# Dividing one late weight transfer into 100 and 28 rows, and moving a one-number load to GpSimd's queue

## The chip, the cores and the metric

The kernel runs on one core of a Trainium2 chip. The metric is device time in microseconds, the median of several executions. A profile of one more execution comes with it; it names the engines PE (TensorE, with PEld for its weight loads), DVE (VectorE), ACT (ScalarE), POOL (GpSimd) and SP (SyncE), and the sixteen DMA engines that move data between main memory and the core's on-chip memory.

## The reference

The computation is one decoding step for two sequences (batch 2, one token each, width 512): a normalised input goes through attention over a window of a cached key and value store, and the result is multiplied by a gate from a small gated network.

```python
xn = layernorm(x)                                     # x: (2, 1, 512)
# attention: 32 query heads, 8 key/value heads, head size 128, the last 4096 of 32768 cached rows
q = (xn @ wq)                                         # wq: (512, 4096)
p = softmax(q k^T * 128 ** -0.5);  o = p v            # k, v: (2, 8, 4096, 128) of the caches
s = o.reshape(2, 1, 4096) @ wo                        # wo: (4096, 512)
# gate
z = gelu(xn @ w_in)                                   # w_in: (512, 1792); z1, z2: halves of 896
g = silu((z1 * (w_sp * layernorm(z2) + b_sp)) @ w_out)  # w_sp, b_sp: one number each; w_out: (896, 512)
out = x + s * g
```

All numbers are 32-bit floats. The windows of k and v are 64 MB together, wq and wo 8 MB each, w_in 3.5 MB and w_out 1.75 MB (MB of 2^20 bytes here).

## The kernel before

Almost all loads are issued by SyncE, in the order of the code: `win`, `wout`, two halves of `wq`, then the eight units (one key/value head each, both sequences) of 4 MB of k and 4 MB of v, interleaved, and at the end eight pieces of `wo`. The large tiles share a ring of four slots of 4 MB; a load into a slot waits until the engine that read the slot's former tile is done. ScalarE issues three small loads at the start (`xs`, the two rows of x, and the two numbers w_sp and b_sp into the tile `wb1`) and the store of the result at the end. GpSimd issues one load, x in another layout (`x4`), after it has cleared that tile, and then prepares constants (`ident`, `selw`, `xnT` and others). The order on TensorE, VectorE, ScalarE and SyncE is that of the code (`InOrder`).

For each unit VectorE transposes the keys in four chunks (`turn`, tiles `kt`), TensorE makes the scores (`scores`), a few short steps on VectorE, TensorE and ScalarE turn them into probabilities (`probabilities`), and TensorE multiplies them with the values (`values`, tile `acc`). The heads' outputs are collected in three sets, of units 0 to 3, 4 and 5, and 6 and 7 (`SETS`), each spread into a tile `oT`.

Each set has its part of `wo`, viewed as 128 rows of 16, 8 and 8 blocks of 512 numbers. It is loaded in pieces: set 0 in two pieces of 8 blocks (2 MB each), set 1 in two of 4 blocks (1 MB each), and set 2 in pieces of 4, 2, 1 and 1 blocks (1 MB, 512 KB, 256 KB, 256 KB). In the code a piece is named by its set `i` and first block `j`; the last but one piece is (2, 6), the last (2, 7). In each piece of one block a row is 2 KB. The products of the first four pieces go to `part`, which is summed into `so`; the products of set 2 are added to `so` directly, piece by piece as they land (the loop over `blocks` from 4 on). Two VectorE instructions then make the result `res`, and ScalarE stores it.

The framework gives each transfer of SyncE and ScalarE one of eight completion counters, in rotation, and a transfer waits until the one before it on its counter has landed.

Of the kernel before, what the change touches and what calls it, by code (L numbers as in the profile page):

```python
# [14 lines left out]
P = 128  # L15
# [27 lines left out]
def kernel(  # L43
# [13 lines left out]
    nc = tc.nc  # L57
    pe, dve, act, sp = (InOrder(tc, e) for e in (nc.tensor, nc.vector, nc.scalar, nc.sync))
# [24 lines left out]
    def slot(name, *shape):  # L83
        return ring.tile([P, *shape], F32, tag="slot", name=name)
# [14 lines left out]
    for a in range(0, KT, 2):  # L99
        t = slot(f"wq{a}", 2, HQ * DH)  # L100
# [1 line left out]
        wqt += [t[:, 0], t[:, 1]]  # L102

    wb1 = cst.tile([1, 2], F32, tag="wb1", name="wb1")
    act.dma_start(wb1[:, 0:1], bass.AP(tensor=w_sp.tensor, offset=w_sp.offset, ap=[[1, 1], [1, 1]]))
    act.dma_start(wb1[:, 1:2], bass.AP(tensor=b_sp.tensor, offset=b_sp.offset, ap=[[1, 1], [1, 1]]))
    x4 = cst.tile([P, DC], F32, tag="x4", name="x4")
    nc.gpsimd.memset(x4, 0.0)
# [381 lines left out]
        scores(cur, 0, 1, 2, 3)  # L490


    wo_s = []
    for kv, n, nj in SETS:
        r0, r1 = kv * REP * DH, (kv + n) * REP * DH
# [2 lines left out]
    for first, of in ((0, (0,)), (1, (1, 2))):  # L498
        t = slot(f"wo{first}", 16, D)
        a = 0  # L500
        for i in of:
            nj = SETS[i][2]
            for j, n in (((0, 8), (8, 8)), ((0, 4), (4, 4)), ((0, 4), (4, 2), (6, 1), (7, 1)))[i]:
                sp.dma_start(t[:, a : a + n, :], wo_s[i][:, j : j + n, :])
                blocks.append((t[:, a : a + n, :], sets[f"oT{i}"][1], j))
                a += n
    EARLY = 24
# [30 lines left out]
    for n in range(4, len(blocks)):  # L538
        t, oT, j = blocks[n]
# [38 lines left out]
```

## Time and profile before

| | |
|---|---|
| median of 3 runs | 218.35 us (218.16 to 218.53) |
| profiled execution | 218.31 us |
| its span, first to last instruction | 216.1 us |
| granted TensorE clock, mean | 0.832 |
| PE / DVE / ACT / POOL busy | 135.0 / 104.9 / 24.0 / 4.0 us |
| read from main memory | 89.40 MB, 414 GB/s over the span |

The profile's times are of one execution and count from its first instruction. A row of an instruction group names its engine, its operation, what it writes and reads (out<-in, buffer numbers left out) and its shape; "idle before" or a bracket is the time in which the engine stood idle just before, and what ended it. Rows of instructions that go through `InOrder` all carry its line, L37. An engine's name with a q means its instruction queue: "SPq DMA_DIRECT2D" is the issue of a transfer, not the transfer. DMA queues are numbered: q1 is SyncE's, q10 ScalarE's, q0 GpSimd's, q8 and q14 carry instructions. In a table of windows each row has the stretch, its length, for each engine the busy time and number of instructions, the granted TensorE clock, the busy share of the sixteen DMA engines and GB/s.

### The profile page before, as it was taken

To read this page: it belongs to the slowest core of one execution; us is meant where nothing else is said; L and a number is where in the kernel's file an instruction comes from. 1 tells how busy PE (TensorE), PEld (TensorE's weight loads), DVE (VectorE), ACT (ScalarE), POOL (GpSimd) and SP (SyncE) were. 2 spreads that over 40 slices of the span, in tenths; PEclk is the share of its full clock that TensorE was granted. 3 is DMA by queue.
4 is the path that set the end of the run, shared out by engine and by line. 5 is a ranking of instruction groups with operands and counts; after the bars stand their busy time and mean duration, and the time that the engine had idled before them with its cause. 6 is when DMAs were issued, how large, how long until landed. Compare 5 with 4: busy or idle time off the path is not lost.

```text
span 216.1 us, 2106 instructions
## 1 busy us (share of the span) xinstructions
PE 135.0 (62%) x862; PEld 42.8 (20%) x862; DVE 104.9 (49%) x161; ACT 24.0 (11%) x60; POOL 4.0 (2%) x20
## 2 busy tenths in 40 slices
PE   0173294627774993973594199179567489968653
PEld 0120021113111221320131023033111122342221
DVE  2604014439539539658508910885784684511201
ACT  4103003200001021101021002012000012031010
POOL 7000000000000000000000000000000000000000
PEclk9998569995588598796589559959966969999998
DMA  7999999999999999999999999999999999999990
GB/s 255 425 437 455 418 455 418 429 431 418 455 400 461 403 455 418 443 425 425 443 421 443 406 449 425 449 425 428 437 418 449 400 456 409 443 409 417 417 373 25
DMA packets 4092, 89.52 MB, mean 414 GB/s; under 512 B 486, under 2 KB 498, under 8 KB 884
## 3 DMA queue, kind: packets, MB, share of 16 engines
q1 hardware_dynamic: 4032, 89.39, 96.7%
q8 instruction: 6, 0.10, 0.2%
q14 instruction: 2, 0.02, 0.0%
q10 hardware_dynamic: 20, 0.01, 0.0%
q0 software_dynamic: 32, 0.00, 0.0%
HBM read 89.40 MB, written 0.00 MB: 414 GB/s over the span
## 4 chain that ended last, share of the span: by engine, by line
DMA 71%; PE 13%; DVE 12%; SPq 1%; ACT 1%; issue 1%; ACTq 0%; DVEq 0%
DMA v<-in_A_v_cache_dram 42%; DMA k<-in_A_k_cache_dram 20%; DMA wo<-in_A_wo_dram 9%; DVE kt L37 8%; PE acc L37 7%; PE s L37 3%; PE pp L37 2%; SPq L37 1%; ACT p L37 1%; DVE pT L37 1%; DVE sm L37 1%; DVE qw L37 1%; DVE both L37 0%; PE col L37 0%; DVE res L37 0%
## 5 line engine op out<-in xcount | busy, mean ns | idle before, releaser
L37 DVE STREAM_TRANSPOSE kt<-k 128x2048 f32<-128x2048 f32 x32 | 72.5, 2286 | 3.5 <-DMA k<-in_A_k_cache_dram 3.5
L37 PE MATMUL acc<-v,pT 128*32 128x512 f32 x256 | 40.1, 781 | 11.4 <-DMA v<-in_A_v_cache_dram 10.5
L37 PE MATMUL s<-kt,qw 128*32 128x512 f32 x256 | 39.8, 669 | 4.6 <-DVE kt L37 4.1
L37 PE MATMUL pp<-p,swap 128*128 128x512 f32 x16 | 12.4, 871 | 21.3 <-ACT p L37 21.3
L37 DVE CUSTOM_DVE_ANT_1 sm<-s,own 128x512 f32<-128x512 f32 x8 | 5.5, 692 | 34.2 <-PE s L37 34.2
L37 PEld LDWEIGHTS acc<-v,pT 128*32 128x32 f32 x256 | 10.5, 152 | 39.4 <-issue 35.6
L37 PE MATMUL q_ps<-wq,xnT 128*32 128x512 f32 x64 | 9.7, 732 | 11.0 <-DMA wq<-in_A_wq_dram 11.0
L37 ACT ACTIVATE o<-acc,diag 128x128 f32<-128x128 f32 x30 | 8.7, 369 | 69.3 <-PE acc L37 68.9
L37 PEld LDWEIGHTS s<-kt,qw 128*32 128x32 f32 x256 | 9.5, 120 | 34.0 <-issue 20.8
L37 ACT ACTIVATE p<-sm,nb 128x512 f32<-128x512 f32 x8 | 5.8, 725 | 70.8 <-DVE nb L37 70.8
L37 DVE TENSOR_TENSOR lsum<-pl,diag 128x4 f32<-128x4 f32 x3 | 0.5, 162 | 16.7 <-PE pl L37 16.7
L37 DVE STREAM_TRANSPOSE pT<-pp 128x512 f32<-128x512 f32 x8 | 5.7, 714 | 5.7 <-PE pp L37 5.6
L37 PE MATMUL z<-win,xnT 128*32 128x448 f32 x32 | 5.7, 887 | 3.9 <-DMA win<-in_B_w_in_dram 3.9
L37 PE MATMUL part<-wo,oT 128*32 128x512 f32 x48 | 6.0, 600 | 2.8 <-DMA wo<-in_A_wo_dram 2.8
L37 PE MATMUL col<-o,selw 128*32 128x128 f32 (+1 forms) x28 | 7.6, 436 | 0.0
L37 PEld LDWEIGHTS pp<-p,swap 128*128 128x128 f32 x16 | 2.8, 218 | 22.0 <-ACT p L37 22.0
L37 PE MATMUL mo<-mg,same 128*128 128x16 f32 x16 | 3.2, 273 | 5.8 <-DVE mg L37 5.3
L37 DVE TENSOR_TENSOR res<-so,gate 128x128 f32<-128x128 f32 x1 | 0.3, 292 | 10.4 <-PE so L37 10.4
L37 ACT ACT_TABLE_LOAD x4 | 5.1, 1283 | 2.0 <-issue 1.9
L37 PE MATMUL xnT_ps<-ident,xn 2*128 2x2 f32 x4 | 0.6, 252 | 7.5 <-DVE xn L37 7.5
L37 PE MATMUL qj_ps<-qT,selj 128*128 128x64 f32 x8 | 2.0, 428 | 4.9 <-DVE qT L37 4.9
L37 PEld LDWEIGHTS q_ps<-wq,xnT 128*32 128x32 f32 x64 | 2.0, 126 | 14.6 <-DMA wq<-in_A_wq_dram 11.1
(110 smaller groups left out, 65.0 us busy)
## 6 DMA issues: line engine op xcount, KB each, us to landing
k<-in_A_k_cache_dram SPq DMA_DIRECT2D x8, 4096.0 KB, 23.4
v<-in_A_v_cache_dram SPq DMA_DIRECT2D x8, 4096.0 KB, 31.2
wq<-in_A_wq_dram SPq DMA_DIRECT2D x2, 4096.0 KB, 28.9
wo<-in_A_wo_dram SPq DMA_DIRECT2D x2, 2048.0 KB
win<-in_B_w_in_dram SPq DMA_DIRECT2D x1, 3584.0 KB, 11.1
wo<-in_A_wo_dram SPq DMA_DIRECT2D x3, 1024.0 KB, 23.2
wout<-in_B_w_out_dram SPq DMA_DIRECT2D x1, 1792.0 KB, 15.0
wo<-in_A_wo_dram SPq DMA_DIRECT2D x1, 512.0 KB, 26.9
```

Source lines behind the costliest of these rows:

```text
L37: return self.tc.keep_in_program_order(call(*args, **kwargs))
```

## The change

The piece (2, 6) of wo is loaded by two transfers, one of its rows 0 to 99 and one of rows 100 to 127, in place of one transfer of 128 rows. The load of w_sp, a single number, is issued by GpSimd instead of ScalarE; in GpSimd's order it stands first, ahead of the clearing of x4. The destinations are the same. The matmuls of the piece now wait for both transfers.

```diff
     wb1 = cst.tile([1, 2], F32, tag="wb1", name="wb1")
-    act.dma_start(wb1[:, 0:1], bass.AP(tensor=w_sp.tensor, offset=w_sp.offset, ap=[[1, 1], [1, 1]]))
+    nc.gpsimd.dma_start(wb1[:, 0:1], bass.AP(tensor=w_sp.tensor, offset=w_sp.offset, ap=[[1, 1], [1, 1]]))
     act.dma_start(wb1[:, 1:2], bass.AP(tensor=b_sp.tensor, offset=b_sp.offset, ap=[[1, 1], [1, 1]]))
...
+    LATE = ((2, 6),)
     wo_s = []
...
             for j, n in (((0, 8), (8, 8)), ((0, 4), (4, 4)), ((0, 4), (4, 2), (6, 1), (7, 1)))[i]:
-                sp.dma_start(t[:, a : a + n, :], wo_s[i][:, j : j + n, :])
+                deal = ((0, 100), (100, P)) if (i, j) in LATE else ((0, P),)
+                for p0, p1 in deal:
+                    sp.dma_start(t[p0:p1, a : a + n, :], wo_s[i][p0:p1, j : j + n, :])
                 blocks.append((t[:, a : a + n, :], sets[f"oT{i}"][1], j))
```

## The prediction

> **What bounds the kernel now.** I read the page first, for the engines, the DMA share and the queues.
>
> ```profile
> span 216.1 us, 2106 instructions
> ...
> DMA  7999999999999999999999999999999999999990
> ...
> ## 3 DMA queue, kind: packets, MB, share of 16 engines
> q1 hardware_dynamic: 4032, 89.39, 96.7%
> q8 instruction: 6, 0.10, 0.2%
> q14 instruction: 2, 0.02, 0.0%
> q10 hardware_dynamic: 20, 0.01, 0.0%
> ...
> DMA 71%; PE 13%; DVE 12%; SPq 1%; ACT 1%; issue 1%; ACTq 0%; DVEq 0%
> ```
>
> The sixteen DMA engines are busy in every slice but the first and the last, and 96.7% of their time goes to one queue, SyncE's. The kernel is bound by the loading of its 89 MB. What ends it is the chain's last part:
>
> ```profile
> 192.53 19.79 DMA wo<-in_A_wo_dram
> ...
> 212.37 0.47 PE so L37 x8
> ...
> 212.87 0.30 DVE res L37
> ...
> 213.19 0.29 DVE res L37
> ```
>
> The last piece of wo lands at 192.53 + 19.79 = 212.32 us. Behind it stand eight matmuls and two VectorE instructions, which the change leaves alone, and then the store and the closing barriers to 216.1. So the time moves with the landing of the last piece, us for us, as long as nothing else becomes late. The profiled execution took 218.31 us, 2.2 us more than its span; I keep these 2.2 us, and the median of the runs, 218.35, is only 0.04 above it.
>
> A transfer has landed when the slowest of its engines has finished. The third view is a table of short windows over the last microseconds, whose last two columns are the busy share of the sixteen engines and GB/s:
>
> ```profile
> 209.60:209.90 0.30, 0.00 (x0) 0.02 (x1) 0.00 (x0) 0.00 (x0) 0.00 (x0) 1.00 0.97 369
> 209.90:210.20 0.30, 0.28 (x12) 0.30 (x16) 0.00 (x0) 0.00 (x0) 0.00 (x0) 1.00 0.60 232
> 210.20:210.50 0.30, 0.30 (x22) 0.30 (x14) 0.00 (x0) 0.00 (x0) 0.00 (x0) 1.00 0.59 225
> 210.50:210.80 0.30, 0.30 (x20) 0.23 (x10) 0.00 (x0) 0.00 (x0) 0.00 (x0) 1.00 0.54 205
> 210.80:211.10 0.30, 0.22 (x12) 0.03 (x4) 0.00 (x0) 0.00 (x0) 0.00 (x0) 1.00 0.46 171
> 211.10:211.40 0.30, 0.30 (x12) 0.30 (x16) 0.00 (x0) 0.00 (x0) 0.00 (x0) 1.00 0.39 150
> 211.40:211.70 0.30, 0.30 (x12) 0.05 (x4) 0.00 (x0) 0.00 (x0) 0.00 (x0) 1.00 0.19 68
> 211.70:212.00 0.30, 0.28 (x11) 0.16 (x8) 0.00 (x0) 0.00 (x0) 0.00 (x0) 1.00 0.02 7
> ```
>
> The engines do not finish together. Some six to eight are done by 210.2 (share 0.6 and then 0.54), the others run on alone, and the last stops after 211.7. Nor does an engine speed up when others stop: 205 GB/s on 0.54 x 16 = 8.6 engines is 23.7 GB/s each, 150 on 0.39 x 16 = 6.2 is 24.0. The area under the shares from 209.9 on is 0.30 x (0.60+0.59+0.54+0.46+0.39+0.19+0.02) = 0.84 us, so sixteen equally loaded engines would all stop at about 210.75 instead of 211.8. About 1.1 us is what any new dealing of the last pieces could gain at most. The queue table names a cause for half of the engines being late: six packets of instructions on queue 8 (0.10 MB, some 16 KB each) and two on queue 14, eight in all, push themselves between the data. If each fell on another engine, eight engines are behind, as the share of 0.54 says, six of them by more.
>
> **The change part by part: the split piece.** How a transfer is dealt out can be counted.
>
> ```profile
> L37 SPq DMA_DIRECT2D k<-in_A_k_cache_dram x8: 534/535/610, 3.0 to 130.8; - x8
> L37 SPq DMA_DIRECT2D v<-in_A_v_cache_dram x8: 534/535/557, 32.3 to 164.3; - x8
> L37 SPq DMA_DIRECT2D wo<-in_A_wo_dram x8: 328/427/1549, 180.7 to 192.5; - x8
> L37 SPq DMA_DIRECT2D wq<-in_A_wq_dram x2: 430/654/877, 1.6 to 2.1; - x2
> L37 SPq DMA_DIRECT2D win<-in_B_w_in_dram x1: 363/363/363, 0.7 to 0.7; - x1
> L37 SPq DMA_DIRECT2D wout<-in_B_w_out_dram x1: 420/420/420, 1.2 to 1.2; - x1
> ```
>
> These are 28 transfers of 128 rows, and 4032 packets are 28 x 16 x 9: each of sixteen engines gets eight rows and one packet more, which must be its completion. The ACT queue's 20 packets fit the same: two rows on two engines (2 + 2), two single numbers (2 x 2), and the output's eight rows on four engines (8 + 4). So rows go evenly to as many engines as divide them. 128 = 16 x 8; 100 has no divisor between 10 and 16, so 10 x 10; 28 = 14 x 2. If both begin at the first engine, engines 1 to 10 get 12 rows of the piece where they had 8, engines 11 to 14 get 2, engines 15 and 16 none. No trace here shows a transfer of 100 rows, so this is an estimate from those counts.
>
> [...]
>
> One row of this piece is 2 KB. Its price comes from the two last pieces, of eight rows an engine each:
>
> ```profile
> 211.07 0.38 PEld L37 LDWEIGHTS so<-wo,oT 128*32 128x32 f32 x16 [0.35 <-DMA wo<-in_A_wo_dram]
> 211.73 0.16 PEld L37 LDWEIGHTS so<-wo,oT 128*32 128x32 f32 x8 [0.28 <-DMA wo<-in_A_wo_dram]
> 212.37 0.16 PEld L37 LDWEIGHTS so<-wo,oT 128*32 128x32 f32 x8 [0.48 <-DMA wo<-in_A_wo_dram]
> ```
>
> The waits for them end at 211.73 and 212.37, 0.64 us apart: 0.08 us a row. (23.7 GB/s an engine would make it 0.086; I take 0.08, the direct reading.) Engines 1 to 10 thus become 4 x 0.08 = 0.32 us later, 11 to 14 become 6 x 0.08 = 0.48 us earlier, 15 and 16 become 0.64 us earlier.
>
> What this does to the end depends on which engines are late, and no view numbers them. If the six hit by queue 8 are the six that are relieved, the last packet moves from 211.8 to about 211.35; the two hit by queue 14, which I put at 211.0 where the share falls from 0.46 to 0.39, move to 211.35 too, and the punctual ones from at most 210.5 to 210.8. The end comes 0.45 us earlier. If the very last engine is one of the first ten, it comes 0.32 us later. Those are the two ends for the split: -0.64 (the last two engines alone being late) to +0.32. I take -0.45: eight packets and eight late engines mean that instruction packets go round the engines instead of returning to one, so a round of six may well fall on six neighbours; and if every queue with little to carry begins at the first engine, as I assumed for these transfers, the low places are less likely to be the late ones. That is a judgement which no row settles, and it gets little more than half of the chances.
>
> TensorE can follow: before 211.73 its weight loads sat idle for 0.28 us and before 212.37 for 0.48 us, both on DMA, so the last eight matmuls could begin up to about 0.7 us earlier. Both halves of the split piece must land before its matmuls. On every engine its share of both halves still comes before its share of the last piece, so the last piece remains the one that ends.
>
> **SyncE's queue.** One more issue costs 0.43 us (median of the wo row) on an engine that only waits. By the order of the built program the completion counters are used in rotation, eight of them; with one more transfer on SyncE the second half waits for the last v, and the last piece waits for the first wo, where before it waited for the last v and went out at 192.5.
>
> ```profile
> 197.45 1.92 PE L37 MATMUL part<-wo,oT 128*32 128x512 f32 x16 [0.63 <-DMA wo<-in_A_wo_dram]
> ```
>
> The first wo ends a wait at 197.45, so the last piece is issued some 5 us later than now and 12 us before the engines begin to run out of work at 209.6. The 6 MB ahead of it cover this: it costs nothing unless that wait lasted to about 208.
>
> **The moved load.** GpSimd issues it ahead of everything else it does; ScalarE has one issue fewer at its start.
>
> ```profile
> 0.74 0.20 POOL L108 MEMSET x<- 128x128 f32 x1 [0.29 <-POOLq L564]
> ...
> 1.30 0.68 POOL L110 DMA_DIRECT2D x<-in_A_x_dram  x1 [0.21 <-POOL ident masks.py:197]
> ...
> 2.41 0.37 DVE L37 TENSOR_REDUCE rowm<-ident 128x32 f32<-128x128 f32 x1 [2.41 <-POOL ident masks.py:199]
> ...
> 11.96 0.23 PEld L37 LDWEIGHTS z<-win,xnT 128*32 128x32 f32 x8 [3.92 <-issue]
> 17.62 0.38 PE L37 MATMUL wb_ps<-wb,ones 1*128 1x2 f32 x2
> ...
> DMA to landing us min/median/max: 6.5/6.5/6.5
> ```
>
> By GpSimd's one issue, 0.68 us, all its memsets, the identity and the load of x4 slip by 0.7 us; behind them waits VectorE's first reduction (2.41) and then the normalised x. TensorE idles 3.92 us before its first use of win, which covers 0.7 us. The number itself lands about 0.74 + 6.5 = 7.2 us (6.5 is what GpSimd's present load of x takes), ten before the matmul at 17.62 that reads it. On the DMA engines a few bytes move from one queue to another; I book 0, within 0.02 us either way. If the cover in front of win were gone, it would cost 0.7 us in the head, still behind a queue with the next loads already in it.
>
> **The sum.** -0.45 (split) + 0 (issues) + 0 (moved load): 218.31 - 0.45 = 217.86 for an execution like the profiled one, 217.9 beside the median of 218.35. About 0.2%, 0.44 us, is what a measurement of this kernel can tell from no change, so even the likeliest case lies on that line.
>
> **The rivals.**
> First, slower: the slowest engine is one of the first ten. Then its 12 rows end 0.32 us later: 218.35 + 0.32 = 218.67. It decides as soon as a single engine among the ten ends within 0.45 us of the last. For it speaks that only six places in sixteen are relieved, so a round of six that starts one engine earlier puts the first-hit engine among the ten; against it that the shares after 211.1 (0.39) show just six engines left, as many as are relieved. [...]
> Second, the split does nothing: the rows are dealt to all engines after all (7 at most and 2, one row more on some: +0.08), or the late engines change from execution to execution and the two signs cancel: 218.35 to 218.45. The three times, 218.16 to 218.53, lie close, which says little either way.
> Third, a confined transfer is worse than counted: as the output's eight rows took four engines, 100 rows could go to four, 25 rows each: 17 more than now, 17 x 0.08 = 1.4 us, so 219.7. Against it stands that the output's other side has only four leading rows.
>
> **How the numbers follow.** Forecast 0.55, slowest among the ten 0.28, nothing 0.09, narrower dealing 0.05, 0.03 for a loss elsewhere. Within the forecast the gain runs from 0.3 to 0.64, and I put 0.38 beyond the line of 0.44 and 0.17 inside. Of the first rival 0.21 stays inside, 0.07 goes beyond. Faster 0.38; same 0.17 + 0.21 + 0.09 = 0.47; slower 0.07 + 0.05 + 0.03 = 0.15. The forecast alone reaches from 217.7 to 218.1; the range of eight in ten goes on to 218.8, over the first rival with its spread, and leaves out the narrower dealing.
>
> **What would show it.** In the changed kernel's windows the share should stay above 0.6 to about 210.6 and then fall within 0.8 us, instead of a tail of 1.9 us; the last two waits on DMA for wo should end about 211.3 and 211.9. Packets of SyncE's queue should be 4032 - 144 + 128 + 10 + 14 = 4040 (two transfers in place of one, 128 rows and 10 + 14 completions), and fewer if fewer engines take part. The forecast is wrong if the last wait ends after 212.37, or if the tail is as long as before.

## The result and the profile after

The changed kernel takes 219.41 us (median; 218.83 to 219.62). The kernel before, run beside it on the same chip, takes 218.53 us (217.71 to 219.09). The ratio is 1.0037, with a 95% interval of 1.0020 to 1.0055: slower by 0.4 to 1.2 us, 0.8 in the middle (the two medians differ by 0.88). The prediction was 217.9 us with a range to 218.8, so it was wrong, on the other side of no change and past the end of the range.

The page of the changed kernel, in the parts that were shown of before:

```profile
span 217.0 us, 2109 instructions
...
DMA  7999999999999999999999999999999999999990
...
## 3 DMA queue, kind: packets, MB, share of 16 engines
q1 hardware_dynamic: 4040, 89.39, 96.8%
q8 instruction: 6, 0.10, 0.2%
q0 software_dynamic: 64, 0.00, 0.0%
q14 instruction: 2, 0.02, 0.0%
q10 hardware_dynamic: 18, 0.01, 0.0%
```

The page hardly differs. SyncE's queue has 4040 packets, the number that was worked out from 10 and 14 engines, and the slices of the DMA engines look as they did. The span is 0.9 us longer. The end of its chain of work shows where (start, duration, what):

```profile
192.40 20.27 DMA wo<-in_A_wo_dram
...
212.80 0.86 PE so L37 x16
...
213.68 0.30 DVE res L37
```

The chain still ends with wo, the matmuls and the result. The transfer that it names, however, is not the last piece. By the order of the code it is the second part of the split piece, rows 100 to 127, which goes out at 192.40 and lands at 212.67. Behind it SyncE has to wait, in a wait that its list of waits before does not have (engine and line, what it waited for, us in total, times, longest):

```profile
SPq L37 <- DMA wo<-in_A_wo_dram: 4.6, 1, 4.6
```

So the last piece goes out at 197.31, where it went out at 192.53 before, and lands 15.8 us later, at 213.1. That is the later issue that the prediction had worked out for it. The chain joins the last sixteen matmuls; the waits in the timeline separate the pieces of wo (start, busy, tile, and in brackets the idle time before and its releaser):

```profile
211.78 0.38 PEld L37 LDWEIGHTS so<-wo,oT 128*32 128x32 f32 x16 [1.02 <-DMA wo<-in_A_wo_dram]
...
212.77 0.19 PEld L37 LDWEIGHTS so<-wo,oT 128*32 128x32 f32 x8 [0.61 <-DMA wo<-in_A_wo_dram]
...
213.19 0.16 PEld L37 LDWEIGHTS so<-wo,oT 128*32 128x32 f32 x8 [0.23 <-DMA wo<-in_A_wo_dram]
```

Before, these three waits ended at 211.07, 211.73 and 212.37. They are now later by 0.71, 1.04 and 0.82 us. The first of them is for the piece of 512 KB that stands ahead of the split piece in the queue, and the change does not touch it. So most of the loss is there before the split piece is needed at all. A dealing of rows that is merely uneven does not do that: in the run with 40 added rows, below, rows queued behind a piece left the waits for the pieces ahead of them where they were (211.02 and 211.66 against 211.07 and 211.73). That engines which had already reached the rows of the split piece slowed down the others is an inference; the windows fit it, though no view shows one engine apart from the others (last two columns: busy share of the sixteen engines, GB/s):

```profile
209.30:209.60 0.30, 0.10 (x4) 0.00 (x0) 0.00 (x0) 0.00 (x0) 0.00 (x0) 1.00 1.06 253
...
209.60:209.90 0.30, 0.00 (x0) 0.00 (x0) 0.00 (x0) 0.00 (x0) 0.00 (x0) 1.00 1.05 239
209.90:210.20 0.30, 0.25 (x9) 0.28 (x13) 0.00 (x0) 0.00 (x0) 0.00 (x0) 1.00 0.93 259
210.20:210.50 0.30, 0.30 (x21) 0.30 (x16) 0.00 (x0) 0.00 (x0) 0.00 (x0) 1.00 0.90 205
210.50:210.80 0.30, 0.30 (x20) 0.26 (x11) 0.00 (x0) 0.00 (x0) 0.00 (x0) 1.00 0.98 253
210.80:211.10 0.30, 0.23 (x11) 0.00 (x0) 0.00 (x0) 0.00 (x0) 0.00 (x0) 1.00 0.84 212
211.10:211.40 0.30, 0.00 (x0) 0.00 (x0) 0.00 (x0) 0.00 (x0) 0.00 (x0) 1.00 0.77 225
211.40:211.70 0.30, 0.00 (x0) 0.00 (x0) 0.00 (x0) 0.00 (x0) 0.00 (x0) 1.00 0.53 191
211.70:212.00 0.30, 0.22 (x8) 0.22 (x12) 0.00 (x0) 0.00 (x0) 0.00 (x0) 1.00 0.35 130
212.00:212.30 0.30, 0.30 (x16) 0.16 (x8) 0.00 (x0) 0.00 (x0) 0.00 (x0) 1.00 0.14 48
```

Read the two last columns together. The share stays near 1 to 210.8, which looks like the even finish that was hoped for. But the bytes do not go with it. Divided by 16 times the share, the rate of a busy engine is 14.2 GB/s at 209.6 (239 / 16.8), 17.4, 14.2, 16.1, 15.8, 18.3, and only from 211.4 on 22.5 and 23.2. Before, it was 23.2 to 24.2 up to 211.4. From 209.3 to 210.8, for 1.5 us, nearly every engine was busy (share 0.90 to 1.06) and moved 14.2 to 17.4 GB/s, some 60 to 75% of its rate before.

### The profile page after: what moved, and what is told of

Its sections match the earlier page's. It is cut to its first block, busy times and chain, and to the rows that moved or that the text cites. A ratio compares the mean times of both kernels' runs of the same rounds, so it can differ in the third digit from the quotient of the medians.

```text
span 217.0 us, 2109 instructions
## 1 busy us (share of the span) xinstructions
PE 136.5 (63%) x862; PEld 42.4 (20%) x862; DVE 104.8 (48%) x161; ACT 24.0 (11%) x60; POOL 4.7 (2%) x21
## 3 DMA queue, kind: packets, MB, share of 16 engines
q1 hardware_dynamic: 4040, 89.39, 96.8%
## 4 chain that ended last, share of the span: by engine, by line
DMA 72%; PE 13%; DVE 11%; issue 1%; SPq 1%; ACT 0%; ACTq 0%; DVEq 0%
DMA v<-in_A_v_cache_dram 42%; DMA k<-in_A_k_cache_dram 20%; DMA wo<-in_A_wo_dram 9%; DVE kt L37 9%; PE acc L37 8%; PE s L37 4%; SPq L37 1%; PE pp L37 1%; DVE sm L37 1%; DVE qw L37 1%; DVE pT L37 1%; PE so L37 0%; ACT p L37 0%; DVE res L37 0%; DVE mg L37 0%
## 5 line engine op out<-in xcount | busy, mean ns | idle before, releaser
L37 PE MATMUL s<-kt,qw 128*32 128x512 f32 x256 | 40.3, 655 | 4.2 <-DVE kt L37 2.9
L37 PE MATMUL q_ps<-wq,xnT 128*32 128x512 f32 x64 | 10.7, 801 | 12.4 <-DMA wq<-in_A_wq_dram 12.4
L37 PE MATMUL part<-wo,oT 128*32 128x512 f32 x48 | 7.4, 725 | 1.8 <-DMA wo<-in_A_wo_dram 1.7
L37 PE MATMUL z<-win,xnT 128*32 128x448 f32 x32 | 4.9, 776 | 3.6 <-DMA win<-in_B_w_in_dram 3.6
L37 PEld LDWEIGHTS mo<-mg,same 128*128 128x128 f32 x16 | 2.4, 188 | 11.9 <-DVE mg L37 11.9
```

The source lines that it names most:

```text
L37: return self.tc.keep_in_program_order(call(*args, **kwargs))
```

## The experiments

Two theories stood at the start. **Crowding** (theory A in the expectations): while the rows of the split piece are written, engines get in each other's way, and lose part of their rate. **Uneven rows** (theory B): by the prediction's count ten engines have 12 rows where they had 8, and one of them is last; that can cost at most the 0.32 us of the prediction's first rival. Beside them stood the moved load (theory C) and the second transfer as such (theory D). In the diffs below, lines with a minus are those of the changed kernel, `P` is 128 and `D` is 512. Every kernel but the first keeps the moved load.

**The two halves of the change, each alone.** The split without the moved load:

```diff
-    nc.gpsimd.dma_start(wb1[:, 0:1], bass.AP(tensor=w_sp.tensor, offset=w_sp.offset, ap=[[1, 1], [1, 1]]))
+    act.dma_start(wb1[:, 0:1], bass.AP(tensor=w_sp.tensor, offset=w_sp.offset, ap=[[1, 1], [1, 1]]))
```

> The split alone, the number's load stays on ScalarE. Theory A (crowding: while the 100 and 28 rows are written, the engines get in each other's way and every packet takes longer): all of the loss is the split's, so about 0.8 us slower than before, the last wait for wo ends near 213.2 us, and between 209.6 and 211.1 us a busy engine moves 14 to 17 GB/s where it moved 24. Theory B (uneven rows alone: ten engines have four rows more): also the split's, but at most 4 x 0.08 = 0.32 us, and a busy engine keeps 24 GB/s. Theory C (the moved load costs it): no loss, within 0.2 us of before.

Measured: 219.37 us (219.06 to 220.74) against 218.16, ratio 1.0061 (1.0036 to 1.0086). The moved load without the split:

```diff
-    LATE = ((2, 6),)
+    LATE = ()
```

> The moved load alone, the piece whole. Theories A and B: within 0.2 us of before, the last wait for wo ends near 212.4 us, first use of win at 12.0 to 12.3 us. Theory C: about 0.8 us slower, as the changed kernel.

Measured: 218.08 us (217.95 to 218.78) against 218.16, ratio 1.0001 (0.9988 to 1.0014). The windows of the split alone, and then the last waits of the moved load alone:

```profile
209.10:209.40 0.30, 0.00 (x0) 0.00 (x0) 0.00 (x0) 0.30 (x1) 0.00 (x0) 0.50 1.05 253
...
209.60:209.90 0.30, 0.15 (x4) 0.15 (x8) 0.00 (x0) 0.10 (x1) 0.00 (x0) 0.50 1.04 239
```

```profile
211.11 0.38 PEld L37 LDWEIGHTS so<-wo,oT 128*32 128x32 f32 x16 [0.36 <-DMA wo<-in_A_wo_dram]
211.76 0.16 PEld L37 LDWEIGHTS so<-wo,oT 128*32 128x32 f32 x8 [0.27 <-DMA wo<-in_A_wo_dram]
212.41 0.16 PEld L37 LDWEIGHTS so<-wo,oT 128*32 128x32 f32 x8 [0.49 <-DMA wo<-in_A_wo_dram]
```

With the split alone the engines are full (1.05) at 15.1 GB/s each; with the moved load alone the waits end within 0.04 us of before. The whole loss is the split's. (In the profile of the split alone the granted TensorE clock was 0.50 at the end, so its last waits are not compared.)

**Even shares, two contiguous halves.** If uneven rows were the cause, 64 + 64 rows would cost nothing, since 64 divides into sixteen fours and by the same count every engine has eight rows again.

```diff
-                deal = ((0, 100), (100, P)) if (i, j) in LATE else ((0, P),)
+                deal = ((0, 64), (64, P)) if (i, j) in LATE else ((0, P),)
```

> The piece in rows 0 to 63 and 64 to 127: every engine gets 4 + 4 rows, as many as in one transfer, so the rows are even. Theory A, in the form that an engine gets consecutive rows and that rows near each other share a way into the memory: each half crowds into half of the ways, 8 rows take up to 16 x 0.08 us, so 0.4 to 0.7 us slower than before, and GB/s per busy engine falls to 12 to 16 while it lasts. [...] Theory B: rows are even, so within 0.1 us of before, 24 GB/s per busy engine. Theory D (a second transfer as such costs it, by its issue, its counter or its completion): as the changed kernel, 0.8 us slower, with 24 GB/s.

Measured: 219.06 us (218.52 to 220.49) against 218.16, ratio 1.0043 (1.0023 to 1.0063). Windows and two waits of it:

```profile
209.10:209.40 0.30, 0.30 (x8) 0.12 (x8) 0.00 (x0) 0.00 (x0) 0.00 (x0) 1.00 0.88 225
209.40:209.70 0.30, 0.10 (x4) 0.00 (x0) 0.00 (x0) 0.00 (x0) 0.00 (x0) 1.00 1.05 225
```

```profile
212.00 0.38 PEld L37 LDWEIGHTS so<-wo,oT 128*32 128x32 f32 x16 [0.88 <-DMA wo<-in_A_wo_dram]
...
212.87 0.46 PEld L37 LDWEIGHTS so<-wo,oT 128*32 128x32 f32 x16 [0.49 <-DMA wo<-in_A_wo_dram]
```

SyncE's queue has 4048 packets, which has room for the 128 rows of the piece and 32 completions: sixteen engines for each half, so eight rows of the piece for each. A busy engine moves 16.0 and 13.4 GB/s. The untouched piece ahead is 0.93 us late (212.00 against 211.07). Uneven rows alone are out as the main cause. The loss, 0.5 to 1.4 us by the interval, is if anything larger than the 0.4 to 0.7 us that crowding was given.

**Uneven shares without the split.** The piece stays whole, and a transfer of 40 rows into a tile that nobody reads follows it: by the prediction's count, 40 = 10 x 4, ten engines get 12 rows in all and the other six keep 8.

```diff
-                for p0, p1 in deal:
-                    sp.dma_start(t[p0:p1, a : a + n, :], wo_s[i][p0:p1, j : j + n, :])
+                sp.dma_start(t[:, a : a + n, :], wo_s[i][:, j : j + n, :])
+                if (i, j) in LATE:
+                    extra = cst.tile([P, 1, D], F32, tag="extra", name="extra")
+                    sp.dma_start(extra[32:72], wo_s[i][32:72, j : j + n, :])
```

> [...] Theory A: no crowding, 24 GB/s per busy engine; the end moves by 0.32 us if the slowest engine is one of the ten, and by 0 to 0.1 us if the slowest are the other six. Theory B (uneven rows cost it all): as the changed kernel, 0.8 us. Theory D: 0.8 us as well.

Measured: 218.38 us (217.97 to 219.48) against 218.16, ratio 1.0013 (0.9998 to 1.0028). Its last waits and a window:

```profile
211.02 0.38 PEld L37 LDWEIGHTS so<-wo,oT 128*32 128x32 f32 x16 [0.38 <-DMA wo<-in_A_wo_dram]
211.66 0.16 PEld L37 LDWEIGHTS so<-wo,oT 128*32 128x32 f32 x8 [0.26 <-DMA wo<-in_A_wo_dram]
212.63 0.16 PEld L37 LDWEIGHTS so<-wo,oT 128*32 128x32 f32 x8 [0.82 <-DMA wo<-in_A_wo_dram]
```

```profile
210.50:210.80 0.30, 0.30 (x16) 0.15 (x7) 0.00 (x0) 0.00 (x0) 0.00 (x0) 1.00 0.60 225
...
212.00:212.30 0.30, 0.08 (x4) 0.00 (x0) 0.00 (x0) 0.00 (x0) 0.00 (x0) 1.00 0.02 7
```

The rate is the old one (225 / 9.6 = 23.4), and the two waits ahead of the last end where they did before (211.07 and 211.73): rows queued behind a piece do not delay it by themselves. The gap between the last two waits is 0.97 us instead of 0.64. That is 0.33 us more, the size that the first rival gave four rows, so in this execution the last engine seems to be among the ten. A share of 0.02 over 0.3 us is 0.1 us of one engine's time, so hardly more than one is left there. That is the size of the uneven rows: 0.3 us, not 0.8.

**Which of the ten.** The piece stays whole, and 8, 9 or 10 rows of 8 KB (four blocks each, to places of `wout` that have been used) follow it, one on each of as many engines if they are dealt as counted: four prices of a 2 KB row on each of 8, 9 or 10 engines. That these are always the first ones is an assumption; no view numbers the engines. The lines stand behind the transfer of the whole piece; with nine and ten rows the slice ends at 68 and 72.

```diff
...
+                if (i, j) in LATE:
+                    some = slice(32, 64, 4)
+                    sp.dma_start(wout[some, 0:4, :], wo_s[i][some, 0:4, :])
```

> [...] It asks where the slowest engine sits: 8 KB take about 0.31 us. The time between the ends of the last two waits for wo is 0.64 us without it. If the slowest engine is one of the first eight it becomes 0.95 us; if all the late ones stand behind the eighth, it stays 0.64 to 0.7 us.

> The same with 9 rows (32, 36 to 64), one for each of the first nine engines. If the gap between the last two waits is 0.95 us here and 0.64 us with eight rows, the slowest engine is the ninth.

> The same with 10 rows (32, 36 to 68), one for each of the first ten engines. The 40 extra rows gave a gap of 0.97 us, so 0.95 us is expected here; 0.64 us would mean that the slowest engine changes from execution to execution. If eight and nine rows leave the gap at 0.64 us and this one makes it 0.95 us, the slowest is the tenth, just inside the ten that the change loads more.

Measured, one time each beside 218.58 of before: 218.23, 218.43 and 218.23. The last waits with eight rows:

```profile
211.40 0.16 PEld L37 LDWEIGHTS so<-wo,oT 128*32 128x32 f32 x8 [0.27 <-DMA wo<-in_A_wo_dram]
212.31 0.16 PEld L37 LDWEIGHTS so<-wo,oT 128*32 128x32 f32 x8 [0.76 <-DMA wo<-in_A_wo_dram]
```

The gap is 0.91 instead of 0.64, so in this execution the last engine seems to be among the eight that got a row more. With nine and ten rows it could not be read, since TensorE came to these pieces later than they landed and waited for none of them. These two are inconclusive.

**A second transfer without other rows.** Two transfers of all 128 rows, each of half the columns (1 KB a row):

```diff
-                deal = ((0, 100), (100, P)) if (i, j) in LATE else ((0, P),)
-                for p0, p1 in deal:
-                    sp.dma_start(t[p0:p1, a : a + n, :], wo_s[i][p0:p1, j : j + n, :])
+                halves = ((0, D // 2), (D // 2, D)) if (i, j) in LATE else ((0, D),)
+                for d0, d1 in halves:
+                    sp.dma_start(t[:, a : a + n, d0:d1], wo_s[i][:, j : j + n, d0:d1])
```

> The piece in two transfers of 128 rows and half the columns (1 KB rows): even rows, the usual way of dealing 128 rows, one transfer more, the counters as in the changed kernel. Theory A (crowding through the way that 100 and 28 rows, or 64 rows, are dealt): within 0.1 us of before, 23 to 24 GB/s per busy engine in the tail. Theory D (a second transfer as such): 0.8 us slower.

> The division by columns once more, since its first measurement came out 0.25% below before. If that was chance: within 0.2% of before. If two transfers of 128 rows end sooner than one: 0.2 to 0.3% faster again, with the last wait for wo near 212.1 us instead of 212.4.

Measured: 217.95 us against 218.58, ratio 0.9975 (0.9957 to 0.9993), and, with the same kernel again, 218.35 against 218.24, ratio 0.9999 (0.9983 to 1.0016). The small gain of the first time did not come back, and nothing is made of it. A second transfer as such costs nothing that can be measured, and neither does the later issue of the last piece: in the kernel of alternate rows, next, which has two transfers as well and loses nothing (1.0007), it goes out at 197.37.

**Halves of alternate rows.** Again 64 + 64 rows and again two transfers, but of the even and the odd rows. If any transfer of fewer than 128 rows were slow, this would be as slow as the contiguous halves.

```diff
-                deal = ((0, 100), (100, P)) if (i, j) in LATE else ((0, P),)
-                for p0, p1 in deal:
-                    sp.dma_start(t[p0:p1, a : a + n, :], wo_s[i][p0:p1, j : j + n, :])
+                deal = (slice(0, P, 2), slice(1, P, 2)) if (i, j) in LATE else (slice(0, P),)
+                for rows in deal:
+                    sp.dma_start(t[rows, a : a + n, :], wo_s[i][rows, j : j + n, :])
```

> The piece in its even and its odd rows, 64 each: even rows, two transfers, as rows 0 to 63 and 64 to 127 were, but each half is spread over the whole height of the memory. [...] Theory A2 (any transfer of other than 128 rows is slow, wherever it writes): as rows 0 to 63 and 64 to 127, 0.7 to 0.9 us and 13 to 15 GB/s.

Measured: 218.33 us (217.85 to 219.51) against 218.24, ratio 1.0007 (0.9990 to 1.0024).

```profile
209.60:209.90 0.30, 0.08 (x4) 0.11 (x8) 0.00 (x0) 0.00 (x0) 0.00 (x0) 1.00 1.02 389
209.90:210.20 0.30, 0.30 (x16) 0.30 (x19) 0.00 (x0) 0.00 (x0) 0.00 (x0) 1.00 0.76 287
```

A busy engine moves 23.8 and 23.6 GB/s, the rate of the whole piece, not the 13 to 15 of theory A2. So it is not the number of rows or of transfers, but which rows go together. Nor is it contiguity as such: the 40 extra rows above, 32 to 71, are contiguous too, and the rate stayed at 23.4. What sets these rows apart from the contiguous halves no run shows.

**The writing side or the reading side.** Contiguous and alternate rows differ at both ends, in the rows of on-chip memory that are written and in the addresses of main memory that are read. Two kernels cross them. One writes contiguous halves from alternate source rows, the other alternate rows from contiguous halves of the source, with `(turns, halves)` in the second line. The lines take the place of the loop over `deal`:

```diff
...
+                whole, halves, turns = (slice(0, P),), (slice(0, 64), slice(64, P)), (slice(0, P, 2), slice(1, P, 2))
+                to, of_ = (halves, turns) if (i, j) in LATE else (whole, whole)
+                for rt, rs in zip(to, of_):
+                    sp.dma_start(t[rt, a : a + n, :], wo_s[i][rs, j : j + n, :])
```

> The piece goes in two transfers that write rows 0 to 63 and 64 to 127, as in the contiguous halves, but read the even and the odd rows of the source (the numbers of this piece land in other rows than they belong to). Writing side crowded: 13 to 17 GB/s per busy engine between 208.8 and 210.5, last wait about 212.8 to 213.2, time +0.6 to +1.0 us over before. Reading side crowded: 23 to 24 GB/s per engine and +0 (within 0.3 us), as with even and odd rows on both sides.

> The other way round: two transfers that write the even and the odd rows, but read rows 0 to 63 and 64 to 127 of the source (the numbers of this piece land in other rows than they belong to). Writing side crowded: 23 to 24 GB/s per engine and +0 (within 0.3 us). Reading side crowded: 13 to 17 GB/s per busy engine and +0.6 to +1.0 us. If both are slow or both are not, neither end alone explains it, and the pairing of the two ends does.

Measured: contiguous writes 219.21 us (218.71 to 219.79) against 218.23, ratio 1.0041 (1.0023 to 1.0058); contiguous reads 218.14 us (217.83 to 219.00) against the same 218.23, ratio 0.9986 (0.9970 to 1.0003). Windows of the first, then of the second:

```profile
209.10:209.40 0.30, 0.30 (x8) 0.06 (x8) 0.00 (x0) 0.00 (x0) 0.00 (x0) 1.00 1.02 232
209.40:209.70 0.30, 0.03 (x4) 0.00 (x0) 0.00 (x0) 0.00 (x0) 0.00 (x0) 1.00 1.03 246
```

```profile
209.10:209.40 0.30, 0.00 (x0) 0.00 (x0) 0.00 (x0) 0.27 (x1) 0.00 (x0) 0.50 1.06 410
209.40:209.70 0.30, 0.27 (x8) 0.22 (x9) 0.00 (x0) 0.00 (x0) 0.00 (x0) 0.50 0.94 362
```

With contiguous writes a busy engine moves 14.2 and 14.9 GB/s, with contiguous reads 24.2 and 24.1. The loss follows the rows that are written, and where the data come from makes no difference that can be measured. This settles the side for halves of 64 rows. For the change's own 100 and 28 rows the two sides were not crossed; that the same is at work there is inferred from the same rates (14 to 18 GB/s) and the same delay of the piece ahead.

**The same split in mid-queue.** The split put on the first 1 MB piece of set 1, with several pieces behind it that could make the loss up:

```diff
-    LATE = ((2, 6),)
+    LATE = ((1, 0),)
```

> The change's 100 and 28 rows on an earlier piece, the third of wo (set 1, block 0, 1 MB, rows of 8 KB, four times as large), the late piece whole. Theory A: both parts of the loss grow with the bytes: up to 4 x 0.32 = 1.3 us from uneven rows, less where no late engine is among the ten, and up to 4 x 0.5 = 2 us from crowding: 1.5 to 3.3 us slower. Theory E (crowding costs only at the tail, where the engines run out of work, and an earlier one is made up by the queue): 0 to 1.3 us.

Measured: 225.79 us (223.26 to 226.00) against 218.24, ratio 1.0313 (1.0273 to 1.0353). Windows of this kernel, and then of before:

```profile
200.00:201.00 1.00, 1.00 (x12) 0.24 (x8) 0.00 (x0) 0.00 (x0) 0.00 (x0) 0.56 1.03 246
...
203.00:204.00 1.00, 0.99 (x17) 0.25 (x9) 0.35 (x1) 0.11 (x1) 0.00 (x0) 1.00 1.14 180
...
208.00:209.00 1.00, 0.37 (x4) 0.00 (x0) 0.00 (x0) 0.00 (x0) 0.00 (x0) 1.00 1.05 270
```

```profile
200.00:201.00 1.00, 0.00 (x0) 0.00 (x0) 0.90 (x5) 0.00 (x0) 0.00 (x0) 1.00 1.05 442
...
203.00:204.00 1.00, 1.00 (x12) 0.13 (x4) 0.00 (x0) 0.00 (x0) 0.00 (x0) 1.00 1.02 426
...
208.00:209.00 1.00, 0.39 (x4) 0.00 (x0) 0.00 (x0) 0.54 (x1) 0.00 (x0) 1.00 0.97 391
```

The wait for the piece behind the split one, first here and then before:

```profile
214.14 0.20 PEld L37 LDWEIGHTS part<-wo,oT 128*32 128x32 f32 x8 [1.94 <-DMA wo<-in_A_wo_dram]
```

```profile
207.33 0.16 PEld L37 LDWEIGHTS part<-wo,oT 128*32 128x32 f32 x8 [2.33 <-DMA wo<-in_A_wo_dram]
```

The loss is not made up, so it does not need the tail; and at 6.0 to 7.7 us by the interval it is about double the 3.3 us that was the most expected of theory A. Full engines move 10 to 16 GB/s each for some nine microseconds, much longer than 1 MB lasts. Most of the loss is in the loads: the piece behind the split one, which the edit leaves alone, is waited for until 214.14 instead of 207.33, 6.8 us later. From there to the first instruction of the result it is 6.8 us (to 220.93) where it was 5.5 (to 212.87); the granted TensorE clock was 0.50 from about 212 on, and the eight matmuls of `so` from `parts` took 0.66 us, where they took 0.43 at a clock of 1.00 before. Why the low rate lasts so long is open.

## Why the prediction was wrong, step by step

- **What bounds the kernel, and that the end follows the last piece of wo**: right. The last three waits moved by 0.71 to 1.04 us, the span by 0.9, the median by 0.88. (The time around the span was 1.8 us in this execution, not the 2.2 that was kept.)
- **The dealing, 100 = 10 x 10 and 28 = 14 x 2**: borne out by the count, 4040 packets, which has room for 24 completions, 10 + 14. Which engines they are no view shows.
- **The price of a row, 0.08 us**: right for whole pieces and for rows added to them (0.33 us for four in the 40-row run). It fails for the split piece, and this is **the step that failed**. The sum took the 0.08 us from transfers of 128 rows and gave it to every engine under the new dealing, as if engines did not touch one another. The remark that an engine does not speed up when others stop could show that only for the dealing of before. With the split a busy engine fell from 23.7 to 14 to 18 GB/s, and the piece ahead, on which the late engines were still at work, came late with the rest. The term that was missing is the +0.71 us on this untouched piece, out of +0.82 on the last wait. None of the rivals contained it.
- **That the six late engines are the six relieved, -0.45**: not borne out. In two executions with added rows the last engine was one of those that got more, ten in one run and eight in the other, as far as the gaps of 0.97 and 0.91 us in place of 0.64 tell. If these are the engines that get more rows in the split too, which is an assumption, even a split whose engines kept their rate would have come out as the first rival, +0.3. Which engine is last in the split kernel itself was not separated.
- **The first rival, 218.67**: its mechanism exists and its size holds (+0.33 us between the last two waits in the 40-row run, where the piece stayed whole). It is not the cause of the loss, which 64 + 64 rows with even shares show as well.
- **The third rival, 100 rows on four engines**: out, by 4040 packets.
- **SyncE's queue and the moved load, 0 each**: right. The last piece went out 4.8 us later, as forecast (about 5), and the alternate rows, whose last piece went out at 197.37, lost nothing (1.0007); the moved load alone gives 1.0001 (0.9988 to 1.0014). The start of the changed kernel's timeline shows the slip behind it:

```profile
1.26 0.68 POOL L105 DMA_DIRECT2D wb<-in_B_w_sp_dram  x1 [0.82 <-POOLq L567]
...
3.51 0.37 DVE L37 TENSOR_REDUCE rowm<-ident 128x32 f32<-128x128 f32 x1 [3.51 <-POOL ident masks.py:199]
...
12.21 0.23 PEld L37 LDWEIGHTS z<-win,xnT 128*32 128x32 f32 x8 [3.66 <-issue]
```

VectorE's first reduction is 1.1 us later (3.51 against 2.41; 0.7 was forecast), and TensorE still idles 3.66 us before its first use of win, so the cover holds.
- **What would show it**: the first half of the test on the share came true, with 0.90 and more to 210.8 where 0.6 to 210.6 was asked, while the kernel got slower. It was a bad test, because it named the share without the bytes. Its second half did not come true: the share then took some 1.7 us to run out, to about 212.5, and not 0.8. The last two waits ended at 212.77 and 213.19 instead of 211.3 and 211.9, and that the last one ended after 212.37 was the sign of being wrong that did its work.

What on the writing side slows the engines is not shown. Contiguous halves ran at 13 to 16 GB/s an engine and alternate rows at 24, and crossing source and destination put the loss on the writing side; the runs go no further than that.

## What to carry to other kernels

Splitting a transfer by rows changes not only how many rows an engine has, but also which rows are written together; here, with contiguous parts, a busy engine fell from 23.7 to 14 to 18 GB/s, and that cost 0.8 us, where the best that the prediction saw in the split was a gain of 0.64, and it reached the piece ahead as well. If a piece has to be split, split its columns or take alternate rows, which cost nothing measurable here on a piece of 256 KB (ratios 0.9975 and 0.9999 for columns, 1.0007 for alternate rows). Judge DMA engines by GB/s per busy engine, the GB/s divided by 16 times the share, because the share alone does not tell a slow engine from a fast one: it was 1.05 beside 239 GB/s here, and 0.97 beside 369 before.

## What was not expected of the hardware

- The sixteen engines were fully busy at about 60% of the rate that they had before: 239 GB/s at a share of 1.05, against 369 GB/s at 0.97.
- In halves of 64 rows, the rate went with the rows of on-chip memory that are written together, not with those that are read: 14.2 GB/s an engine with contiguous halves written, 24.2 with contiguous halves read.
- Splitting a piece delayed the piece queued ahead of it, by 0.71 us here and by 0.93 us with 64 + 64 rows. That this goes through engines that are ahead of others is inferred.
- The single number loaded through GpSimd's queue took 32 packets (64 in place of 32 in all), against 2 on ScalarE's queue (18 in place of 20), and its issue 0.68 us.
